# Turning a block's rows on the vector engine instead of TensorE, with the rows fetched in four partition groups and the later w1 loads issued by ScalarE

## The chip, the cores and the metric

The kernel runs on one core of a Trainium2 chip. The metric is the device time of one execution in microseconds; smaller is better. The core has five engines that run side by side: TensorE (PE in the profile; PEld is its weight load), VectorE (DVE), ScalarE (ACT), GpSimd (POOL) and SyncE (SP). SP computes nothing: it reads table entries into registers and issues DMA transfers. ScalarE and GpSimd can issue transfers too. Each engine works through its own instructions strictly in the order in which the program lists them, and waits on semaphores for the others.

## The reference

Two stages follow each other. The first is an attention without softmax: `q` and `k` are sketched into 64 features each, and the output is a ratio. The second is a mixture of experts: a noisy router picks two of eight experts for each of 4,352 rows, and each expert is a two-layer perceptron.

```python
def phi(x):
    a = np.einsum('rd,bhsd->bhsr', S1, x)
    b = np.einsum('rd,bhsd->bhsr', S2, x)
    return np.einsum('bhsi,bhsj->bhsij', a, b).reshape(*x.shape[:-1], r * r)
q_p, k_p = (phi(q), phi(k))
kv = np.einsum('bhsf,bhsd->bhfd', k_p, v)
z = np.sum(k_p, axis=2)
num = np.einsum('bhsf,bhfd->bhsd', q_p, kv)
den = np.einsum('bhsf,bhf->bhs', q_p, z)[..., None] + 1e-06
attn = num / den                     # 4 batches, 4 heads, 1088 rows, 32 wide
x = attn.transpose(0, 2, 1, 3).reshape(4352, 128)
...
noisy_logits = x @ w_gate + np.log1p(np.exp(x @ w_noise)) * noise
top2 = the two largest of the 8, top2_w = their softmax
for e in range(8):                   # w1[e] is 128 x 1024, w2[e] is 1024 x 128
    h = np.maximum(x[mask] @ w1[e], 0.0)
    out[mask] += top2_w[mask, k, None] * (h @ w2[e])
```

All of it is in float32.

## The kernel before

**Attention and router.** The four batches are worked through in turn. For each, TensorE turns and sketches k and q, VectorE multiplies the features, and a router step (`router`) finds the two experts of each row. The weight of the pick and the attention's denominator are multiplied into the row at once, so what a block later works on is already weighted. GpSimd scatters the rows, 128 at a time (L638), into a DRAM table `xs` that is sorted by expert. A row there is 129 words: 128 values and, as the last word, the id of the pair of row and expert.

**Blocks.** A block is 128 neighbouring rows of `xs` that belong to one expert. There are 72 in this part of the program, in six waves; a wave can begin as soon as enough rows have been routed. VectorE writes for each wave a small table `tab`, from which the expert and the first row of each block are read into a register (`value`, L762). With the order of blocks in the trace counted from 0, the waves begin at blocks 0, 5, 9, 17, 27 and 43.

For block b, `work_off` lists:
- `fetch_rows(b + 2)`: a load of 128 x 129 words from `xs` into a tile `xb`, issued by SP (L804). There are 11 such tiles; one is free again when GpSimd has scattered the block's result by the ids in the last column.
- `fetch_weights(b + 3)`: a load of the expert's w1, 128 x 1024 words, issued by SP (L796). There are four tiles; one is free again when TensorE has done its block.
- eight matmuls in two groups of four, w1 by the turned rows `bT`, into the PSUM tile `hp` (L981). In float32 each takes two slots of TensorE, so a group has 8. `hp` has two buffers. Each group is evicted through a ReLU into `h`: by ScalarE (L778), or, from block 27 on, the second group by VectorE (L776).
- `turn_input(b + 1)`, listed after the first of the two groups: TensorE transposes the 128 x 128 values of the next block's `xb` into PSUM (L885), and ScalarE copies them to the SBUF tile `bT` (L778).
- `second()`, two groups behind: the matmuls of `h` by w2, which stays in SBUF, into `acc` (L896). After a block's second one, `acc` is copied to `y` and GpSimd scatters it into the DRAM table `parts` (L929).

**Order.** The order on TensorE, ScalarE, VectorE and SP is the one in which the program lists the instructions (`manual_schedule`). Until block 27 or so the blocks are interleaved with attention and routing of later batches, step by step. While the last wave of rows is made ready, SP also writes eight pads of 128 x 129 words into `xs` (L767), one per block. In the last dozen blocks SP loads finished pairs from `parts` (`two`, L1036), VectorE adds the two halves of each row, and ScalarE and SP store them to `out` (L1042).

**Semaphores of transfers.** Transfers issued by SP and ScalarE share eight semaphores, which are given out in turn; a transfer waits for the earlier one that used the same semaphore.

Of the kernel before, what the change touches and what calls it, by code (L numbers as in the profile page):

```python
# [21 lines left out]
def kernel(  # L22
# [14 lines left out]
    nc = tc.nc  # L37
    V = nc.vector
    P = nc.NUM_PARTITIONS
    B, H, S, DH = q.shape  # L40
    R = S1.shape[0]
    D = H * DH
    E = moe_w_gate.shape[1]
# [23 lines left out]
    XW = D + 1  # L67
# [61 lines left out]
    ident = const.tile([P, P], F32, name="ident")  # L129
# [131 lines left out]
    xs = dram.tile([E * CAP + P, XW], F32, name="xs", tag="xs")  # L261
# [71 lines left out]
    def behind(name, i, step):  # L333

        for s_, writers in steps[name].items():
            if s_ > step:
                tc.declare_no_dep(i.ins, group=f"{name}{s_}", reason="rows of later steps")
            else:
                for w in writers:
                    tc.add_manual_dep(i.ins, w.name, SYNC, reason="reads what they write")  # L340
        tc.add_to_no_dep_group(name, i.ins)
# [303 lines left out]
    def send_all(step):  # L645
        send(sum(w[0] <= step for w in waiting))
# [111 lines left out]
    SP, PE, DVE, ACT, POOL = (getattr(mybir.EngineType, x) for x in ("SP", "PE", "DVE", "Activation", "Pool"))  # L758
    SPARE = 3

    def value(tab, w, at, most, engine=SP):
        return nc.values_load(tab[0:1, w, at:at + 1], engines=[engine], min_val=0, max_val=most,  # L762
                              skip_runtime_bounds_check_because="counts of pairs, clamped in the table")
# [6 lines left out]

    combining = {}
    W_AHEAD, X_AHEAD, LAG = 3, 2, 2

    def evict(o, i, vector, relu=False):
        if vector:
            V.tensor_scalar_max(o, i, 0.0) if relu else V.tensor_copy(o, i)  # L776
        else:
            nc.scalar.activation(out=o, in_=i, func=AF.Relu) if relu else nc.scalar.copy(o, i)  # L778

    def work_off(*waves, skip=0, most=None, at=None):  # L780
# [8 lines left out]
        weights, rows, ready, later = {}, {}, {}, []  # L789

        def fetch_weights(i):
            if i < n:
                tab, k = tabs[blocks[i][0]], blocks[i][1]
                w1 = weights[i] = wpool.tile([P, F], F32, name="w1", tag="w1")
                e = value(tab, 0, k, E - 1)
                nc.sync.dma_start(w1[:], moe_w1[bass.ds(e, 1), :, :].rearrange("o p f -> p (o f)"))  # L796

        def fetch_rows(i):
            if i < n:
                tab, (k, step) = tabs[blocks[i][0]], blocks[i][1:3]  # L800
                send_all(step)
                r = value(tab, 1, k, E * CAP)
                xb = rows[i] = xpool.tile([P, XW], F32, name="xb", tag="xb")
                behind("xs", nc.sync.dma_start(xb[:], xs[bass.ds(r, P), :]), step)  # L804

        def late(i):

# [74 lines left out]

        def turn_input(i, acc):

            nc.tensor.transpose(acc[:, P:2 * P], rows[i][:, 0:D], ident[:])  # L885
            xT = moe.tile([P, P], F32, name="bT", tag="bT")
            evict(xT[:], acc[:, P:2 * P], False)
            ready[i] = (xT, value(tabs[blocks[i][0]], 0, blocks[i][1], E - 1, PE))

        def accumulator():  # L890
            return ps_o.tile([P, 512], F32, name="acc", tag="acc")
# [49 lines left out]
        def combine_some(k):  # L941
# [15 lines left out]
            if k == LAST - SPARE - LATE - 1:  # L957
                combining["last"], = combine(last_parts[:, NT - FINAL:NT], last_out[:, NT - FINAL:NT], 2, FINAL, nc.sync, 1)
                next(combining["last"])

        fetch_weights(0)
        for i in range(X_AHEAD):
            fetch_rows(i)
        for i in range(1, W_AHEAD):
            fetch_weights(i)
        acc = accumulator()
        turn_input(0, acc)
        yield
        for b in range(n):

            for i in range(b + X_AHEAD, b + X_AHEAD + 1 + min(max(b - (n - 2 * LATE - 4), 0), LATE)):
                if i not in rows:
                    fetch_rows(i)
            fetch_weights(b + W_AHEAD)
            if b:
                acc = accumulator()
            w1, (xT, e), spread = weights.pop(b), ready.pop(b), blocks[b][3]
            for j0 in range(0, FJ, 4):
                hp = ps_h.tile([P, 512], F32, name="hp", tag="hp")
                for j in range(4):  # L980
                    nc.tensor.matmul(hp[:, P * j:P * (j + 1)], lhsT=w1[:, P * (j0 + j):P * (j0 + j + 1)],  # L981
                                     rhs=xT[:], start=True, stop=True)
                h = hpool.tile([P, 512], F32, name="h", tag="h")
                evict(h[:], hp[:], spread and j0 > 0, relu=True)
                later.append((acc, h, e, j0, b))
                if len(later) > LAG:
                    second()
                if j0 == 0 and b + 1 < n:
                    turn_input(b + 1, acc)
                at[0] = blocks[min(n - 1, b + 1 + W_AHEAD)][0] if j0 else 0  # L990
                yield
# [361 lines left out]
```

## Time and profile before

| | |
|---|---|
| time, median of 3 runs | 388.0 us (384.33 to 388.43) |
| the profiled run | 369.02 us, span on the core 367.1 us |
| TensorE busy | 349.4 us, 95% |
| VectorE, ScalarE, GpSimd busy | 155.6, 127.1 and 155.6 us (42%, 35%, 42%) |
| granted TensorE clock | 0.99 |
| turns of blocks on TensorE (L885) | 72, listed with 275 ns each |
| copies of the turned rows by ScalarE | 72, 265 ns each |
| loads of rows issued by SP | 72, 64.5 KB each |
| loads of w1 issued by SP | 72, 512 KB each |

The profile is a recording of one execution. Its page has the busy time of each engine, the span in 40 slices with the busy share in tenths, the DMA queues, and the costliest groups of instructions (line, engine, operation, tiles, how many; then busy time and mean ns of one; then the idle time of the engine just before them and who ended it). Matmuls overlap, so the listed time of one is longer than the distance to the next. Further views of the same recording give the instructions of one tile, all instructions in order of time (start, duration, engine, line, with the idle time before them in brackets), and the busy time of each engine in chosen stretches.

### The profile page before, as it was taken

Reading aid. Unit: us, or ns where it says so; the run is one execution under the profiler, and the core shown is the slowest. Engines: PE = TensorE matmul, PEld = TensorE weight load, DVE = VectorE, ACT = ScalarE, POOL = GpSimd, SP = SyncE. Lnnn points to the kernel's source line nnn. Section 1 sums busy time; section 2 is a strip of 40 time slices with the busy share of each in tenths; the row PEclk is TensorE's granted clock in tenths of the full one; section 3 lists DMA queues with packets and bytes.
Section 4 is the critical chain, followed back from the end, with each engine's and each line's share of the span. In section 5 each row is a group of like instructions: output and inputs, shape, how many; then the busy total and the mean of one; then the engine's idle time right before and its main releaser. Section 6 shows DMA issues by size and latency. Waiting matters only on the chain. (4 is left out here: it accounts for less than half of the span.)

```text
span 367.1 us, 9385 instructions
## 1 busy us (share of the span) xinstructions
PE 349.4 (95%) x3064; PEld 343.5 (94%) x3064; DVE 155.6 (42%) x557; ACT 127.1 (35%) x314; POOL 155.6 (42%) x216
## 2 busy tenths in 40 slices
PE   7998879999999999999999999999999999999990
PEld 7887779999999999999999999999999999999990
DVE  4759979335355160086602323232222222334650
ACT  3353342545544445554442121212222222222220
POOL 7002740367454577463756654323232323232352
PEclk9999998999999999999999999999999999999997
DMA  6799737657274465556588775656565657979651
GB/s 188 196 273 294 209 99 249 203 156 236 55 213 138 131 171 175 155 178 170 165 242 246 219 212 181 194 166 199 157 196 166 192 168 209 321 220 342 230 179 48
DMA packets 47231, 71.04 MB, mean 194 GB/s; under 512 B 10143, under 2 KB 32290, under 8 KB 47184
## 3 DMA queue, kind: packets, MB, share of 16 engines
q1 hardware_dynamic: 39216, 59.71, 55.3%
q0 software_dynamic: 4608, 9.07, 7.2%
q10 hardware_dynamic: 3360, 1.64, 1.5%
q8 instruction: 28, 0.46, 0.5%
q14 instruction: 19, 0.16, 0.1%
HBM read 58.25 MB, written 12.56 MB: 193 GB/s over the span
## 5 line engine op out<-in xcount | busy, mean ns | idle before, releaser
L981 PE MATMUL hp<-bT,w 128*128 128x128 f32 x1152 | 154.1, 277 | 0.0
L896 PE MATMUL acc<-w,h 128*128 x1152 | 152.0, 275 | 0.0
L981 PEld LDWEIGHTS hp<-bT,w 128*128 128x128 f32 x1152 | 140.9, 193 | 0.5
L896 PEld LDWEIGHTS acc<-w,h 128*128 128x128 f32 x1152 | 140.1, 192 | 0.0
L929 POOL DMA_INDIRECT parts<-y,xb x68 | 69.8, 1026 | 147.3 <-DVE y L776 79.0
L778 ACT ACTIVATE h<-hp 128x512 f32<-128x512 f32 x99 | 59.1, 597 | 143.3 <-PE hp L981 133.8
L638 POOL DMA_INDIRECT xs<-xg,to x68 | 70.1, 1030 | 46.1 <-DVE co L562 25.6
L776 DVE TENSOR_SCALAR h<-hp 128x512 f32<-128x512 f32 x45 | 31.1, 692 | 109.0 <-PE hp L981 109.0
L778 ACT COPY bT<-acc 128x128 f32<-128x128 f32 x72 | 19.1, 265 | 25.5 <-PE acc L885 25.1
L382 DVE TENSOR_TENSOR phi<-ab 128x1024 f32<-128x1024 f32 (+1 forms) x18 | 20.5, 1137 | 0.6
L885 PE MATMUL acc<-ident,xb 128*128 128x128 f32 x72 | 19.8, 275 | 0.9 <-DMA xb<-xs 0.9
L776 DVE COPY y<-acc 128x128 f32<-128x128 f32 x41 | 12.0, 292 | 10.4 <-PE acc L896 9.9
L418 PE MATMUL bank<-vld,phi 128*128 128x96 f32 x128 | 15.7, 280 | 0.5 <-DVE phi L382 0.5
L418 PEld LDWEIGHTS bank<-vld,phi 128*128 128x128 f32 x128 | 15.4, 198 | 0.6 <-DVE phi L382 0.6
L362 PE MATMUL bank<-sk,xT 128*128 128x128 f32 x102 | 13.6, 281 | 1.2 <-ACT xT L357 0.8
L362 PEld LDWEIGHTS bank<-sk,xT 128*128 128x128 f32 x102 | 12.3, 194 | 1.8 <-ACT xT L357 1.3
L778 ACT COPY y<-acc 128x128 f32<-128x128 f32 x30 | 8.0, 265 | 13.0 <-PE acc L896 13.0
L377 DVE TENSOR_TENSOR ab<-bank,ab 128x256 f32<-128x256 f32 (+1 forms) x15 | 5.6, 374 | 15.4 <-ACT ab L369 15.4
L504 DVE TENSOR_SCALAR den<-nd 128x16 f32<-128x16 f32 (+2 forms) x5 | 0.9, 179 | 25.1 <-ACT nd L478 25.1
L576 DVE TENSOR_TENSOR xg<-nd,co 128x256 f32<-128x256 f32 (+2 forms) x20 | 11.3, 605 | 0.5 <-issue 0.2
L885 PEld LDWEIGHTS acc<-ident,xb 128*128 128x128 f32 x72 | 10.4, 145 | 1.1 <-DMA xb<-xs 1.1
L357 ACT COPY xT<-bank 128x512 f32<-128x512 f32 (+1 forms) x15 | 7.5, 526 | 7.4 <-PE bank L355 7.4
(204 smaller groups left out, 262.1 us busy)
## 6 DMA issues: line engine op xcount, KB each, us to landing
w<-in_moe_w_dram SPq DMA_DIRECT2D x72, 512.0 KB
xb<-xs SPq DMA_DIRECT2D x72, 64.5 KB
two<-parts SPq DMA_DIRECT2D x8, 384.0 KB
kld<-in_k_dram SPq DMA_DIRECT2D x4, 512.0 KB
qld<-in_q_dram SPq DMA_DIRECT2D x4, 512.0 KB
vld<-in_v_dram SPq DMA_DIRECT2D x8, 256.0 KB
out_dram<-two ACTq DMA_DIRECT2D x8, 192.0 KB
xs<-xg,to POOLq DMA_INDIRECT x68
```

The lines of the kernel that those rows point to most:

```text
L357: nc.scalar.copy(self.xT[:, 0:P * self.n], ps[:, 0:P * self.n])
L362: nc.tensor.matmul(ps[:, P * i:P * (i + 1)], lhsT=self.xT[:, P * i:P * (i + 1)], rhs=sk[:].rearrange("p i h y -> p (i h y)"), start=True, ...
L382: yield V.tensor_tensor(out=self.phi[:, 0:n].rearrange("p t h (i j) -> p (t h) i j", i=R), in0=th[:, :, 0, :].unsqueeze(3).to_broadcast([P ...
L418: nc.tensor.matmul(ps[:, W * hp:W * (hp + 1)], lhsT=lhsT, rhs=rhs, start=(t == 0 and hp == 0), stop=(t == NT), skip_group_check=True)
L576: return V.tensor_tensor(out=xg[:, i, 0:n, 2 * DH * hp:2 * DH * (hp + 1)].rearrange("p t (h d) -> p t h d", h=2), in0=x[:, :, hp, 0:2 * (D ...
L638: x = nc.gpsimd.indirect_dma_start(out=xs[:], out_offset=bass.IndirectOffsetOnAxis(ap=to[:, i, t:t + 1], axis=0), in_=xg[:, i, t, :], in_o ...
L776: V.tensor_scalar_max(o, i, 0.0) if relu else V.tensor_copy(o, i)
L778: nc.scalar.activation(out=o, in_=i, func=AF.Relu) if relu else nc.scalar.copy(o, i)
L885: nc.tensor.transpose(acc[:, P:2 * P], rows[i][:, 0:D], ident[:])
L896: nc.tensor.matmul(acc[:, 0:D], lhsT=h[:, P * j:P * (j + 1)], rhs=w2[:, bass.ds(FJ * e + (j0 + j), 1), :], start=(j0 + j == 0), stop=(j0 + ...
L929: sent = nc.gpsimd.indirect_dma_start(out=parts[:], out_offset=bass.IndirectOffsetOnAxis(ap=rows.pop(i)[:, D:XW].bitcast(U32), axis=0), in ...
L981: nc.tensor.matmul(hp[:, P * j:P * (j + 1)], lhsT=w1[:, P * (j0 + j):P * (j0 + j + 1)], rhs=xT[:], start=True, stop=True)
```

## The change

The turn of a block's rows leaves TensorE. VectorE can turn squares of 32 x 32 values inside a tile, in place of the whole 128 x 128. So that this gives the full turn, the rows are fetched in another order: the load of one 128 x 129 piece becomes four, each of which fills 32 partitions. Partition 32i + b of `xb` then holds, for j = 0 to 3, columns 32i to 32i + 31 of row 32j + b. Each run of 32 values is 128 bytes. When VectorE turns each of the sixteen squares in place, the tile is the transpose of the rows. A fifth load fetches the ids into the last column as before. TensorE has 72 transposes less, and ScalarE 72 copies from PSUM to SBUF less.

As SP now issues five transfers for a block's rows, the loads of w1 are issued by ScalarE, except for those of the first three blocks of each wave, whose table may not be ready yet.

```diff
+    TURN = 32
...
                 w1 = weights[i] = wpool.tile([P, F], F32, name="w1", tag="w1")
-                e = value(tab, 0, k, E - 1)
-                nc.sync.dma_start(w1[:], moe_w1[bass.ds(e, 1), :, :].rearrange("o p f -> p (o f)"))
+                engine, queue = (ACT, nc.scalar) if k >= W_AHEAD else (SP, nc.sync)
+                e = value(tab, 0, k, E - 1, engine)
+                queue.dma_start(w1[:], moe_w1[bass.ds(e, 1), :, :].rearrange("o p f -> p (o f)"))
...
                 xb = rows[i] = xpool.tile([P, XW], F32, name="xb", tag="xb")
-                behind("xs", nc.sync.dma_start(xb[:], xs[bass.ds(r, P), :]), step)
+                x = xs[bass.ds(r, P), :]
+                for i_ in range(P // TURN):
+                    c = slice(TURN * i_, TURN * (i_ + 1))
+                    behind("xs", nc.sync.dma_start(xb[c, 0:D].rearrange("b (j a) -> b j a", a=TURN),
+                                                   x[:, c].rearrange("(j b) a -> b j a", b=TURN)), step)
+                behind("xs", nc.sync.dma_start(xb[:, D:XW], x[:, D:XW]), step)
...
         def turn_input(i, acc):
-            nc.tensor.transpose(acc[:, P:2 * P], rows[i][:, 0:D], ident[:])
             xT = moe.tile([P, P], F32, name="bT", tag="bT")
-            evict(xT[:], acc[:, P:2 * P], False)
+            V.transpose(xT[:], rows[i][:, 0:D])
             ready[i] = (xT, value(tabs[blocks[i][0]], 0, blocks[i][1], E - 1, PE))
```

In the program that results, each turn on VectorE waits for the landings of its four pieces. It stands where the copy stood in the order: after the eviction of the first group of the block before.

## The prediction

> **What bounds the kernel now.** I read the page's busy times and slices first, then the windows, then the timeline of one block in the middle of the longest wave.
>
> ```profile
> PE 349.4 (95%) x3064; PEld 343.5 (94%) x3064; DVE 155.6 (42%) x557; ACT 127.1 (35%) x314; POOL 155.6 (42%) x216
> PE   7998879999999999999999999999999999999990
> L885 PE MATMUL acc<-ident,xb 128*128 128x128 f32 x72 | 19.8, 275 | 0.9 <-DMA xb<-xs 0.9
> ```
> ```profile
> 188.00:340.00 152.00, 152.00 (x1364) 152.00 (x1363) 43.07 (x93) 36.32 (x85) 53.59 (x54) 1.00 0.71 214
> ```
> ```profile
> 234.44 0.27 PE L885 MATMUL acc<-ident,xb 128*128 128x128 f32 x1
> 234.44 0.97 PEld L981 LDWEIGHTS hp<-bT,w 128*128 128x128 f32 x8
> 234.55 1.06 PE L981 MATMUL hp<-bT,w 128*128 128x128 f32 x8
> 234.75 0.27 ACT L778 COPY bT<-acc 128x128 f32<-128x128 f32 x1 [0.34 <-PE acc L885]
> ...
> 235.63 0.33 SPq L796 DMA_DIRECT2D w<-in_moe_w_dram  x1
> ...
> 236.71 0.33 SPq L804 DMA_DIRECT2D xb<-xs  x1
> ...
> 238.12 0.27 PE L885 MATMUL acc<-ident,xb 128*128 128x128 f32 x1
> ```
>
> TensorE has no gap from 55 us, where the first block starts, to 351 us, where the last one does: it is the bound, and all else lies beside it. The timeline gives its true price. The turn (L885) is listed with 0.27 us, but the next matmul starts 0.11 us after it, and a block repeats every 3.68 us (234.44 to 238.12) with 33 slots (16 L981, 16 L896, one turn): 3.68/33 = 0.1115 us a slot. So the 19.8 us of the group are not 19.8 us of time.
>
> **What the Trainium skill says.** "Trainium Kernel Development and Optimization", Performance Expectations, calls matmul busy time a bad metric because matmuls are pipelined; the trace agrees (275 ns listed, 111 ns apart). "VectorE: DVE Perf Modes", The three transpose paths: the vector engine turns 32x32 squares only, 311 ns for 128x128 in bf16; no row of this trace shows the instruction. "DMA: Bandwidth & Descriptors", Issuing engines are not separate DMA queues: a second issuing engine saves only the issuing sequencer's time; here an issue takes 0.33 us. The same page, Specifications, wants 512 B or more a piece for line rate. The trace's packet records agree in direction: 28 ns for a 516 B packet, 13 ns for 128 B, 9 ns for 4 B.
>
> **The change part by part.**
>
> Removed from TensorE: 72 turns of 0.1115 us = 8.0 us, all on the path. A block becomes 3.57 us.
>
> Removed from ScalarE: 72 copies of 0.265 us = 19.1 us. It was 24% busy from 188 us on: no time. Added to it: 54 w1 loads (the first three of each of six waves stay on SP), each a table read (0.27 us on SP), register work and an issue (0.38 us for its out_dram stores), about 0.9 us. Behind such a load on ScalarE stands the eviction of h (0.60 us), and hp has two buffers, so TensorE waits for it only 2.65 us after hp is done (three groups of 8 slots). 0.9 + 0.6 fits; the load's buffer is freed by a group of matmuls that ends 1.8 us before this hp. In the last dozen blocks the load also waits for landings of SP's transfers; this I price with the end phase below.
>
> Added to VectorE: 72 turns. Nearest rows: 0.29 us for a 128x128 copy; the skill's 0.31; at half rate for four-byte elements 0.6. I take 0.3: 21.6 us on an engine that is 42% busy, 28% in the long wave (43.07 of 152): hidden. Each waits for four landings, and behind it stand router steps and, from block 27 on, the eviction of h's second half. TensorE needs the result three groups (2.65 us) later. VectorE's bursts between two turns stay under that except in the last table (five steps of 0.94 us): 0.3 us.
>
> Transfers: a block's rows were 128 packets of 516 B, 128 x 28/16 = 0.22 us on each of 16 engines; they become 512 of 128 B and 128 of 4 B, (512 x 13 + 128 x 9)/16 = 0.49 us. 0.27 us more of 3.57 us on a DMA share of 0.71 gives 0.79: hidden. If each 128 B packet took as long as a 516 B one, +0.75 us, 0.92: still hidden.
>
> Added to SP, where the cost is: five issues a block in place of one.
>
> ```profile
> L804 SPq DMA_DIRECT2D xb<-xs x72: 332/333/564, 53.0 to 330.9; - x72
> ```
> ```profile
> L187 SPq DMA_DIRECT2D v_rest<-in_v_dram x8: 595/611/617, 4.2 to 42.7; - x8
> ```
> ```profile
> L200 SPq DMA_DIRECT2D wgn<-in_moe_w_noise_dram x2: 425/426/426, 9.9 to 10.4; - x2
> ```
> ```profile
> 182.47 0.52 SPq L804 DMA_DIRECT2D xb<-xs  x1
> 183.56 0.33 SPq L796 DMA_DIRECT2D w<-in_moe_w_dram  x1
> 184.39 0.36 SPq L767 DMA_DIRECT2D xs<-pad  x1
> 185.31 0.34 SPq L804 DMA_DIRECT2D xb<-xs  x1
> ```
>
> The first three lines give minimum, median and maximum of the issue in ns. A 128-row load costs 0.333; v_rest has the new pieces' 128 packets of 128 B but 64 rows, 0.611; wgn has their 32 rows, 0.35 to 0.43. The fourth is SP's own order in a wave start: each transfer with its table read costs about 0.88 us. **The unknown is the issue of one piece, p, between 0.333 and 0.611 us.** 32 rows are the nearer likeness, and other loads of wgn's time also took 0.42 to 0.51 where later ones of their shape took 0.33, so I take p = 0.38. A piece without a table read adds about 0.16 us of register and semaphore work (37 + 29 + 17 ns and gaps). A block's rows then cost SP (0.86 - 0.333 + p) + 3 (p + 0.16) + 0.49 = 3.0 us. That is under 3.57 only because w1 left SP; with w1 it would be 3.9. SP no longer stands behind w1's wait for TensorE, so it can run ahead: in the middle of a wave nothing is lost. What is lost is at the places where SP starts without a lead:
> - Block 0: TensorE already waits for xb (0.9 us). Three more pieces, 1.6 us, less what TensorE can do meanwhile: 1.0.
> - Blocks 5 and 6: rows first at 78.1 us, TensorE at 83.0; the four pieces are usable at 81.9; block 6 just in time: 0.
> - Blocks 27 to 34: eight pads stand between, and w1 of the first three stays on SP. Rows of 27 issued from 182.5 to 185.0, then twice 0.88 + 0.88 + 3.0 and five times 3.9: 214.0. A load is usable some 1.5 us after its issue (block 0: 53.0 to 54.8), the turn takes 0.3, and the id is not waited for: 215.3. TensorE would be there at 188.5 + 7 x 3.57 = 213.5: 1.8.
> - The end phase, 12 loads of two among the last rows (18 us of lead before): 0.5.
>
> Sum: -8.0 + 0.3 + 1.0 + 1.8 + 0.5 = -4.4 us. The timed runs are 1.05 times the profiled one (388.0 against 369.0 us); scaled, -4.6 us: **383.4 us.**
>
> **The rivals.**
> - *All is hidden:* p is 0.333 to 0.35, or SP's lead suffices. For it: 32-row loads down to 0.35. -8.0 x 1.05: 379.6 us.
> - *The gain is given back in waits for rows:* p = 0.43, as wgn's median. Rows 3.2 us a block; blocks 27 to 34 lose 3.4, block 0 1.2, the end 2.5, VectorE's order 1: 8.1 against 8.0, so 388 us.
> - *SP becomes the bound, slower:* p = 0.54, as 64-row loads of two (0.51 to 0.58). Rows cost 3.66 us, over TensorE's 3.57, and SP never regains a lead. Rows of 27 end at 185.5, two blocks of 5.42, five of 4.54, 37 of 3.66, 8 us for two: 362.4, usable 363.7, where TensorE starts its last block at 351.4 now: +12.3, scaled 401 us. At 0.611 the same sum gives +25, 414 us. For it: every 64-row load is slow, so issue time isn't packets alone. Against: wgn.
>
> **How the numbers follow.** Forecast 0.40, all hidden 0.13, given back 0.21, SP the bound 0.26. Of the forecast's spread a fifth lies within 1%. Faster by over 1% (under 384.1): 0.48. Within 1%: 0.23. Slower: 0.29, SP's case and a tail of given back. The range runs from 378.5, just under all hidden, to 401, SP's middle case; its upper half up to 414 is left out, with some 0.05 below.
>
> **What would show it.** Right: a repeat of 3.57 us a block, no L885, a turn on VectorE near 0.3 us, xb issues of 0.33 to 0.43 us, and TensorE's idle gaps, waiting for VectorE's turn and behind it for xb, near blocks 0 and 27 to 34 only, 3 to 4 us in all. Wrong: xb pieces of 0.5 us or more with SP issuing without pause and a block at SP's pace; or ScalarE's h held up by its w1 loads and TensorE waiting for hp; or a turn of over 0.6 us.

## The result, and the profile after

The changed kernel takes 416.4 us (median of four runs, 413.3 to 422.0), the kernel before beside it 386.2 us. The ratio is 1.075, with a 95% interval of 1.063 to 1.087: slower by 30 us, where 4.6 us less were forecast. Ratios leave out runs that took over 1.5% longer than the fastest of the same kernel, here the one of 422.0.

The page of the kernel after, its busy times, its slices, and the groups that answer to those of before (the first line is the first-layer matmuls of the kernel before):

```profile
L981 PE MATMUL hp<-bT,w 128*128 128x128 f32 x1152 | 154.1, 277 | 0.0
```
```profile
PE 363.6 (87%) x2992; PEld 352.6 (85%) x2992; DVE 173.2 (42%) x629; ACT 106.0 (25%) x242; POOL 153.3 (37%) x216
...
PE   8998679978999996999996889999989799885792
...
PEclk9997769998999996999998999999999999999698
...
L989 PE MATMUL hp<-bT,w 128*128 128x128 f32 x1152 | 159.9, 283 | 28.2 <-issue 16.3
...
L779 ACT ACTIVATE h<-hp 128x512 f32<-128x512 f32 x99 | 58.9, 598 | 208.1 <-PE hp L989 89.4
...
L895 DVE STREAM_TRANSPOSE bT<-xb 128x128 f32<-128x128 f32 x72 | 22.0, 306 | 80.7 <-DMA xb<-xs 66.1
```

TensorE no longer runs in one piece: the row of nines of before now has sixes, sevens and eights among the blocks, and the first-layer matmuls (L989) stand 28.2 us idle where they stood 0.0. The last group tells who is late: the turn itself is short (306 ns), but VectorE idles 66.1 us ahead of it for rows. Next the issues of the rows (minimum, median and maximum in ns; L811 are the four pieces, L813 the ids), and the windows of the stretch that was shown of before (columns: sum, PE, PEld, DVE, ACT and POOL busy, clock, DMA share, GB/s):

```profile
L811 SPq DMA_DIRECT2D xb<-xs x288: 3/317/1567, 52.5 to 383.5; - x144
...
L813 SPq DMA_DIRECT2D xb<-xs x72: 11/352/1235, 55.0 to 384.1; - x72
```
```profile
188.00:340.00 152.00, 138.19 (x1187) 135.02 (x1187) 49.41 (x139) 27.28 (x51) 55.75 (x56) 0.99 0.67 176
```

A piece costs SP 0.317 us, less than forecast, and the DMA share is 0.67 against 0.71: no single issue is dear, and the DMA engines are not full. In the timeline a block in an undisturbed place repeats after 3.57 us, as worked out:

```profile
262.69 1.06 PE L989 MATMUL hp<-bT,w 128*128 128x128 f32 x8
...
266.26 0.94 PE L989 MATMUL hp<-bT,w 128*128 128x128 f32 x7
```

The waits (engine, tile and line, what ended them; us in total, how often, longest) show two chains, the first of transfers into the turn, the second of transfers into ScalarE's evictions. In the kernel before ScalarE's evictions had only these of any length behind transfers:

```profile
ACT h L778 <- DMA out_dram<-two: 5.6, 2, 3.1
...
ACT h L778 <- DMA w<-in_moe_w_dram: 2.5, 1, 2.5
```

In the kernel after:

```profile
DVE bT L895 <- DMA xb<-xs: 66.1, 27, 6.2
...
ACT h L779 <- DMA xb<-xs: 34.4, 9, 5.4
...
ACT h L779 <- DMA w<-in_moe_w_dram: 22.3, 7, 4.1
...
PE hp L989 <- ACT h L779: 8.4, 8, 2.2
```

An eviction needs neither rows nor weights. It waits because a w1 load stands ahead of it on ScalarE, and that load waits for an earlier transfer on its semaphore. The timeline shows one such case:

```profile
301.27 0.35 ACTq L799 DMA_DIRECT2D w<-in_moe_w_dram  x1
...
301.73 0.60 ACT L779 ACTIVATE h<-hp 128x512 f32<-128x512 f32 x1 [4.94 <-DMA xb<-xs]
...
302.37 1.16 PE L989 MATMUL hp<-bT,w 128*128 128x128 f32 x8 [1.56 <-ACT h L779]
```

The w1 load has the semaphore of a piece that SP issued at 298.16 us and that landed at 301.14. Only then is it issued. The eviction follows 3.6 us after the last matmul of its `hp` ended (298.13 in the same timeline), and TensorE has lost 1.56 us.

**The account.** The changed kernel is compared with another profile of the kernel before from a chip of like speed (a_before below). From the first block to the last group of first-layer matmuls it takes 337.9 us against 304.5, 33.4 more. Gaps of TensorE are 36.6 us against 6.3: +30.3. (A gap is here the distance from the start of one matmul to the start of the next, less one slot of 0.1115 us, so it is a little longer than the idle time that a view lists.) By the work that ended last before each gap, some 18 us of them are behind the turn and some 13 behind ScalarE's h. The clock is at half for 20.5 us of the stretch (windows at 94.7, 159.6 to 166.4, 224.4 and 384.9 to 391.7) against none. TensorE stands still in 2.7 us of that, and half of the rest is lost: about +9. The turns removed: 72 x 0.1115 = -8.0. The sum is about +31; the other 2 us stay unaccounted for. By place, the larger gaps of the kernel after are 4.8 us at 85 to 110, 4.0 at 155 to 160 (2.2 of such gaps were there before), 9.1 at 180 to 250, 7.0 at 280 to 335 and 10.5 at 360 to 390.

Some chips ran the kernel before in 386 to 388 us and others in 367; each ratio is to the kernel before on the same chip, and times of different chips are not set against each other.

### The profile page after: what moved, and what is told of

It is laid out like the page before. It is cut to its first block, busy times and chain, and to the rows that moved or that the text cites. A ratio compares the mean times of both kernels' runs of the same rounds, so it can differ in the third digit from the quotient of the medians.

```text
span 416.0 us, 10178 instructions
## 1 busy us (share of the span) xinstructions
PE 363.6 (87%) x2992; PEld 352.6 (85%) x2992; DVE 173.2 (42%) x629; ACT 106.0 (25%) x242; POOL 153.3 (37%) x216
## 4 chain that ended last, share of the span: by engine, by line
PE 62%; DMA 10%; issue 9%; DVE 7%; SPq 6%; ACT 2%; another core or an unknown queue 1%; POOL 1%; ACTq 0%; DVEq 0%; POOLq 0%
PE hp L989 24%; PE acc L904 21%; PE bank L418 5%; SPq L811 4%; DMA xb<-xs 4%; DMA w<-in_moe_w_dram 3%; PE bank L475 2%; PE bank L362 2%; PE acc L475 2%; DMA late<-parts,mates 1%; PE acc L458 1%; DMA two<-parts 1%; PE bank L458 1%; ACT h L779 1%
## 5 line engine op out<-in xcount | busy, mean ns | idle before, releaser
L989 PE MATMUL hp<-bT,w 128*128 128x128 f32 x1152 | 159.9, 283 | 28.2 <-issue 16.3
L989 PEld LDWEIGHTS hp<-bT,w 128*128 128x128 f32 x1152 | 144.0, 196 | 33.2 <-issue 22.0
L904 PE MATMUL acc<-w,h 128*128 x1152 | 155.5, 279 | 0.0
L904 PEld LDWEIGHTS acc<-w,h 128*128 128x128 f32 x1152 | 143.5, 196 | 0.2 <-issue 0.2
L895 DVE STREAM_TRANSPOSE bT<-xb 128x128 f32<-128x128 f32 x72 | 22.0, 306 | 80.7 <-DMA xb<-xs 66.1
L382 DVE TENSOR_TENSOR phi<-ab 128x1024 f32<-128x1024 f32 (+1 forms) x18 | 20.5, 1137 | 0.6
L418 PE MATMUL bank<-vld,phi 128*128 128x96 f32 x128 | 18.5, 311 | 0.5 <-DVE phi L382 0.5
L475 PE MATMUL bank<-kv,phT 128*128 128x98 f32 (+1 forms) x72 | 10.1, 303 | 3.7 <-issue 3.7
L475 PEld LDWEIGHTS bank<-kv,phT 128*128 128x128 f32 (+1 forms) x72 | 9.3, 213 | 4.2 <-issue 4.0
L475 PE MATMUL acc<-kv,phT 128*128 128x98 f32 (+1 forms) x72 | 9.5, 299 | 0.8 <-ACT kv L442 0.5
L475 PEld LDWEIGHTS acc<-kv,phT 128*128 128x128 f32 (+1 forms) x72 | 9.2, 212 | 1.1 <-ACT kv L442 0.6
```

The costliest lines, as they stand in the source:

```text
L382: yield V.tensor_tensor(out=self.phi[:, 0:n].rearrange("p t h (i j) -> p (t h) i j", i=R), in0=th[:, :, 0, :].unsqueeze(3).to_broadcast([P ...
L418: nc.tensor.matmul(ps[:, W * hp:W * (hp + 1)], lhsT=lhsT, rhs=rhs, start=(t == 0 and hp == 0), stop=(t == NT), skip_group_check=True)
L475: nc.tensor.matmul(ps[rows, c0:c0 + YC], lhsT=self.phT[hp][:, P * i + rows.start:P * i + rows.stop], rhs=kv[:, hp, :], start=True, stop=True)
L895: V.transpose(xT[:], rows[i][:, 0:D])
L904: nc.tensor.matmul(acc[:, 0:D], lhsT=h[:, P * j:P * (j + 1)], rhs=w2[:, bass.ds(FJ * e + (j0 + j), 1), :], start=(j0 + j == 0), stop=(j0 + ...
```

## The experiments

In the table are all kernels, in order of the transfers that a block needs (rows and ids, and w1), as SP and ScalarE issue them from a wave's fourth block on.

| kernel | SP + ScalarE | what | ratio (95%) |
|---|---|---|---|
| before | 2 + 0 | | 1 |
| b_one_load_w_sp | 2 + 0 | turn on VectorE, one load of rows | 0.988 (0.982 to 0.992) |
| c_one_load_w_act | 1 + 1 | the same, w1 by ScalarE | 0.988 (0.984 to 0.992) |
| f_sixteen | 2 + 0 | one load, sixteen single squares | 1.210 (1.199 to 1.221) |
| i_two_w_act | 2 + 1 | two loads of 64 rows | 0.996 (0.993 to 0.999) |
| r_every_second | 2 or 6, + 0 | the change in 19 of 72 blocks | 0.997 (0.994 to 0.999) |
| j_four_w_act | 4 + 1 | four loads of 32 rows with ids | 1.039 (1.032 to 1.046) |
| d_four_plain_w_act | 5 + 1 | the change, whole rows | 1.081 (1.076 to 1.086) |
| g_first_whole | 5 + 1 | one load of rows, four small ones after it | 1.073 (1.065 to 1.080) |
| after; m_after_again | 5 + 1 | the change | 1.075; 1.075 (1.071 to 1.078) |
| h_w_after_h; n_h_again | 5 + 1 | w1 listed behind h | 1.080; 1.085 (1.079 to 1.090) |
| q_x_ahead | 5 + 1 | rows four blocks ahead | 1.071 (1.062 to 1.079) |
| t_ids_pool | 5 + 1 | copies of ids off VectorE | 1.095 (1.092 to 1.099) |
| o_split_w_act | 3 + 3 | two pieces by ScalarE | 1.079 (1.072 to 1.086) |
| p_split_w_sp | 4 + 2 | the same, w1 by SP | 1.043 (1.035 to 1.051) |
| s_split_ahead | 4 + 2 | p with rows four blocks ahead | 1.043 (1.036 to 1.050) |
| e_four_w_sp | 6 + 0 | all by SP | 1.128 (1.120 to 1.136) |

**The parts alone.** First the kernel before again, for a second profile; then the turn on VectorE with one load of whole rows, w1 by SP (b) or by ScalarE (c). Both leave out the exchange of squares, so `bT` holds each square turned but in the wrong place. Against the changed kernel:

```diff
-                for i_ in range(P // TURN):
...
-                behind("xs", nc.sync.dma_start(xb[:, D:XW], x[:, D:XW]), step)
+                behind("xs", nc.sync.dma_start(xb[:], xs[bass.ds(r, P), :]), step)
```

> The kernel before, once more, for its profile. The two profiles at hand differ by 10 us before the first block starts (first L981 or L989 matmul at 56.0 and 66.2 us), in a part of the program that the change doesn't touch, with half the TensorE clock granted for 17 us of the changed kernel's first 61 us and for 3.4 us of the other's. If that is chance, this profile shows windows of half clock too, at other places than the first one, and a span between 367 and 387 us. If it belongs to the change, the first block starts at 56 us again with a clock of 0.99.

> The turn on VectorE alone: rows in one load as before, w1 issued by SP as before. Left out: the exchange of the squares outside the diagonal, so the rows that the matmuls see are permuted. What every theory expects: TensorE loses 72 slots of 0.1115 us and nothing is added to SP, so 8 us less than before, ratio 0.98, block repeat 3.57 us. If a turn on VectorE or its place in the order costs by itself, the ratio is 1.0 or more.

> As b_one_load_w_sp, with the later w1 loads issued by ScalarE; the same part is left out. Theory A (w1's issue on ScalarE, standing before the eviction of h, is what costs): 10 to 20 us over b_one_load_w_sp, with TensorE waiting for ScalarE's h. Theory B (it costs only because five small transfers a block use up the eight semaphores, so that w1's issue waits for recent landings): with two transfers a block the wait is for a landing four blocks back, so within 2 us of b_one_load_w_sp. Theory C (late landings of rows alone): the same as b_one_load_w_sp.

Measured: 383.3 us for the kernel before (one run), 381.1 for b and 381.1 for c beside 385.7. The turn's move is worth 1.2%, 4.6 us, and ScalarE's issuing of w1 costs no time as long as there are two transfers a block. All of the loss comes with the four pieces and the load of ids. ScalarE's evictions are held in c too, for 13.8 us behind transfers of rows, but too briefly to stop TensorE for long; the changed kernel has 34.4 and 22.3 (w1). The turn waits for rows for 9.9 us, where the changed kernel has 66.1:

```profile
ACT h L779 <- DMA xb<-xs: 13.8, 4, 3.7
...
DVE bT L890 <- DMA xb<-xs: 9.9, 3, 5.7
```

**Packets or the number of transfers.** d takes the four loads and the id load, but each loads 32 whole rows; j drops the id load from that, i has two loads of 64 rows with their ids. All three leave out the exchange.

```diff
-                    behind("xs", nc.sync.dma_start(xb[c, 0:D].rearrange("b (j a) -> b j a", a=TURN),
-                                                   x[:, c].rearrange("(j b) a -> b j a", b=TURN)), step)
+                    behind("xs", nc.sync.dma_start(xb[c, 0:D], x[c, 0:D]), step)
```

> As the changed kernel, but each of the four loads takes 32 whole rows (32 packets of 512 B in place of 128 of 128 B); the exchange of squares is left out as in b_one_load_w_sp. If the number of transfers is what costs (theories A, B and C): within 8 us of the changed kernel, ratio 1.05 to 1.08 to before. If the size of the packets costs (theory D): most of the loss goes, ratio under 1.02.

> As d_four_plain_w_act, with two loads of 64 whole rows, ids included, so three transfers a block with w1's in place of six; the exchange of squares is left out. Eight semaphores then reach back over 2.7 blocks and SP's cost is about 1.7 us a block. Theories B and C alike: as c_one_load_w_act, ratio 0.985 to 0.995. If each further transfer costs its landing on the path: about 8 us over c_one_load_w_act, a quarter of the way to d_four_plain_w_act.

> Four loads of 32 whole rows, the ids in them: five transfers a block in place of d's six. The exchange of squares is left out. If every further transfer costs alike, and two loads (three transfers) were 0.996 and d (six) 1.081, five transfers give 1.05 on a straight line from three. If there is a knee where the rows' issues pass what a wave start or the semaphores leave, it is under 1.03. If the id load alone is dear (128 packets of 4 B), also under 1.03.

d is as slow as the changed kernel, with packets of 512 bytes in place of 128: packets are not the cause. Three transfers a block give 0.996, five 1.039, six 1.07 to 1.08. j lies a little under the straight line from three to d (1.053), so the last transfer seems to cost more than the ones before it; i, j and d ran on three different chips, and the intervals of j and of the line nearly touch. "DMA: Bandwidth & Descriptors", Rules for kernel authors, of the Trainium skill, says to join many small transfers, since under 64 KB one pays mostly overhead. The runs agree: by the packet records a 16 KB piece is 128 x 13 ns / 16 = 0.1 us of data, and lands 2.8 us after its issue (median; nine in ten within 4.1).

**Late pieces or SP's pace.** In g the block's own rows come in one load, first; four loads of 32 x 32 follow into a tile that nothing reads. The exchange is left out.

```diff
+                behind("xs", nc.sync.dma_start(xb[:], x[:]), step)
+                spare = spool.tile([P, TURN], F32, name="spare", tag="spare")
...
+                    behind("xs", nc.sync.dma_start(spare[c, :], x[c, 0:TURN]), step)
-                behind("xs", nc.sync.dma_start(xb[:, D:XW], x[:, D:XW]), step)
```

> A block's rows come in one load of 128 whole rows with their ids, the first of the block; four small loads of 32 x 32 into a buffer that nothing reads follow it, so a block has six transfers again (five by SyncE, w1 by ScalarE), but the block's own rows no longer land last. The exchange of squares is left out. If SyncE's pace and the shared completion semaphores cost the time (a transfer has to wait for the landing of an earlier one): about as d, ratio 1.06 to 1.09, with VectorE's turns waiting some 20 us for rows. If it is the late landing of a block's last piece: near c, 0.99 to 1.01. If it is the small packets or the bytes: near c as well, since the small loads carry little.

1.073: transfers that nobody waits for, with hardly any bytes, cost as much as the pieces. What costs is that they are issued at all.

**All issues on SP, and w1 behind the eviction.** e is the changed kernel with every w1 on SP. h and n list the w1 load behind the first eviction of h, and m repeats the changed kernel beside n.

```diff
-            fetch_weights(b + W_AHEAD)
...
                 evict(h[:], hp[:], spread and j0 > 0, relu=True)
+                if j0 == 0:
+                    fetch_weights(b + W_AHEAD)
```

> The changed kernel with all w1 loads issued by SP, as before. A block then costs SP 3.0 + 0.9 = 3.9 us, over TensorE's 3.57. Theory C (SP's pace and landings): slower than the changed kernel by 0.3 to 0.5 us for each of 45 blocks, 10 to 25 us, ratio 1.10 to 1.14, with all gaps ending at the turn. Theory B (ScalarE's wait is the greater part): 5 to 12 us faster than the changed kernel.

> The changed kernel with the w1 load listed behind the eviction of h's first group instead of ahead of it. In the changed kernel's blocks TensorE's gaps sum to 36.6 us: 18.1 end with VectorE's turn, 12.8 with ScalarE's eviction of h. Theory B (the w1 load, waiting for a landing on a shared semaphore, holds up the eviction behind it): the 12.8 us go and most of them come back as time, 8 to 13 us less than the changed kernel, ratio about 1.05. Theory C (SP's pace and the rows' landings set the blocks' pace and the held eviction only hides it): within 4 us of the changed kernel.

> The changed kernel again, for the same chip as the next one and for a profile of another execution: ratio 1.075 to 1.10. TensorE's gaps among the blocks: some 37 us, half of them behind VectorE's turns and a third behind ScalarE's h.

> The changed kernel with a w1 load listed behind the first eviction of h, beside the changed kernel on one chip. If ScalarE's held evictions are a part of the loss of their own: 0.02 to 0.03 under the changed kernel's ratio (12.8 us of TensorE's gaps are theirs). If they only stand in for the late rows: within 0.01 of it.

e is slowest but one, 1.128: with six issues SP is behind almost everywhere, and the turn waits 139.6 us for rows. Another 12.6 us of TensorE's gaps, after 354 us, wait for w1 itself, which SP now issues there among the combine's loads.

```profile
DVE bT L895 <- DMA xb<-xs: 139.6, 51, 5.7
```

The changed kernel repeats (1.075). n is not faster than m but slower, 1.085 against 1.075. In the two profiles TensorE's gaps behind ScalarE fall from 13.0 to 9.6 us, and those behind the turn rise from 21.3 to 25.7. But the edit didn't free the evictions: they stand behind rows and w1 for 37.0 + 7.7 us in m and for 42.0 + 29.4 in n. So this pair doesn't tell whether held evictions are a part of the loss of their own.

**SP or the shared semaphores.** o and p keep the six transfers and their semaphores, but ScalarE issues two of the four pieces (o), and SP gets all w1 back (p). q changes only how far ahead rows are listed; s does this to p.

```diff
+                x2 = xs[bass.ds(value(tab, 1, k, E * CAP, ACT), P), :]
...
-                    behind("xs", nc.sync.dma_start(
+                    queue, x = (nc.sync, x) if i_ < 2 else (nc.scalar, x2)
+                    behind("xs", queue.dma_start(
...
```
```diff
-    W_AHEAD, X_AHEAD, LAG = 3, 2, 2
+    W_AHEAD, X_AHEAD, LAG = 3, 4, 2
```

> The changed kernel with two of a block's four pieces issued by ScalarE: as many transfers over the same completion semaphores, but SyncE issues three a block and ScalarE three (its w1 load among them). If SyncE's own pace is what costs the time: ratio 0.98 to 1.02, SyncE idle again for a third of the long wave. If the semaphores and landings shared by six transfers a block cost it: 1.06 to 1.09, as the changed kernel. If ScalarE's issues now hold up h: 1.03 to 1.06, with TensorE's gaps behind ScalarE's h.

> The same split, with every w1 load on SyncE: four transfers a block there, two on ScalarE. If SyncE's pace decides: between o and the five-transfer kernel (1.039), 1.00 to 1.04. If the semaphores decide: 1.06 to 1.09 again.

> The changed kernel with rows listed four blocks ahead in place of two. If the loss is SyncE's order, rows standing behind its waits for w1 and for the combine's loads near the end (some 13 us there): 1.04 to 1.05. If it is SyncE's pace, which an order cannot change: 1.07 to 1.08.

> The split of p_split_w_sp (two pieces by ScalarE, every w1 by SyncE) with rows listed four blocks ahead. If the late rows and ScalarE's held evictions are two parts that add: p without the turns' 9 us, 1.01 to 1.03. If they stand for one another, as with q_x_ahead: 1.04 to 1.06, with the gaps behind ScalarE's h.

Only s does what one of its expectations said (1.04 to 1.06, gaps behind ScalarE's h); o has the ratio of one and the gaps of another, p lies just above its range, and q hits a range for another reason. In o the gaps behind the turn fall to 3.3 us at most, as SP's pace would have it, but those behind ScalarE's h rise to 28.7: the ratio stays. The waits of o, then of p, then of q:

```profile
ACT h L779 <- DMA xb<-xs: 118.0, 34, 7.3
...
DVE bT L897 <- DMA xb<-xs: 39.3, 17, 5.9
```
```profile
ACT h L779 <- DMA xb<-xs: 69.5, 21, 6.9
...
DVE bT L897 <- DMA xb<-xs: 65.6, 33, 5.8
```
```profile
ACT h L779 <- DMA xb<-xs: 58.7, 18, 6.5
...
ACT h L779 <- DMA w<-in_moe_w_dram: 24.6, 8, 4.4
...
DVE bT L895 <- DMA xb<-xs: 6.3, 5, 2.7
```

In q the turn hardly waits (6.3 us, 66.1 in the changed kernel), ScalarE waits more, and the ratio is the same, 1.071. That equality is in part chance. At the second block TensorE stands 6.1 us for a w1 load that SP now issues behind the rows of two more blocks, and 10.2 us at half clock begin there:

```profile
PE hp L989 <- DMA w<-in_moe_w_dram: 6.1, 1, 6.1
```

The first three blocks take 26.1 us in q and 18.7 in t (below), on the same chip. Part of what earlier rows gained is given back there, so the equal ratio doesn't show that the loss only changed its place.

In s as in p the ratio is 1.043, with the gaps behind the turn down from 6 us to 2 and those behind ScalarE's h up from 10 to 12. So there are two costs, and moving issues trades one for the other. On SP, in the long wave, it is the issuing itself: in the 129 us from 205 to 334 SP waits for only 5.8 us in the changed kernel, 0.9 in m and 6.5 in e, and rows come late because five or six issues a block take its time. On ScalarE it is the wait for landings: an issue stands still until the earlier transfer on its semaphore has landed, and evictions stand still behind it. The division has a better and a worse point: 4 + 2 is better than 5 + 1, 3 + 3 and 6 + 0. No run changed the number of semaphores, so what more of them would give is not shown.

**Single squares.** f keeps one load, all w1 on SP, and turns sixteen squares one by one straight to their places.

```diff
-            V.transpose(xT[:], rows[i][:, 0:D])
+            for r in range(0, P, TURN):
+                for c in range(0, D, TURN):
+                    V.transpose(xT[c:c + TURN, r:r + TURN], rows[i][r:r + TURN, c:c + TURN])
```

> Rows in one load, w1 by SP, and VectorE turns the sixteen squares one by one, each to its own place, so the whole reference is computed. If a square takes about 0.1 us beside its neighbours, VectorE has 1.6 us more a block, 2.6 of 3.57 us in the long waves, and the kernel is as b_one_load_w_sp or up to 8 us over it: ratio 0.99 to 1.01. If it takes 0.19 us, as the smallest dependent steps of the router, VectorE needs 4 us a block and becomes the bound: ratio 1.06 or more.

```profile
L892 DVE STREAM_TRANSPOSE bT<-xb 32x32 f32<-32x32 f32 x1152 | 233.2, 202 | 16.0
```

One square takes 202 ns, all sixteen of a tile in one instruction 306. In this profile (of a run of 452.8 us; the three others took 443.0 to 449.6) VectorE is busy 141.1 of the 152 us from 188 to 340, with a block every 4.4 us in the long wave: it has become the bound.

**The end phase.** The largest gap of the changed kernel, 4.9 us before block 68, has VectorE standing at copies of the ids of the last four blocks, which wait for landings and stand ahead of that block's turn. t gives these copies to GpSimd.

```diff
-                    V.tensor_copy(one(ids, late(i)), rows[i][:, D:XW].bitcast(U32))
+                    nc.gpsimd.tensor_copy(one(ids, late(i)), rows[i][:, D:XW].bitcast(U32))
```

> The changed kernel with the copies of the last four blocks' ids (one column each) made by GpSimd in place of VectorE. In the changed kernel they stand ahead of the turn of block 68 on VectorE, wait for the ids of blocks 68 to 71 until 386 us, and TensorE has a gap of 4.9 us there. If the turn's place behind VectorE's own waits costs that: the gap goes and the half clock behind it, 5 to 8 us less, ratio 1.054 to 1.062. If the rows would be late anyway: 1.07 to 1.08, with the gap behind block 68's rows.

A miss: 1.095. The single gap is gone, but the last blocks have five gaps of 0.6 to 2.0 us behind the turn in its place, 6.5 us in all. They stand behind VectorE's additions for the combine, which wait for their own loads from SP (6.6 and 4.9 us in two cases). Why the ratio is above the 1.071 that q had on this chip stays open; the changed kernel itself was not run on it.

**A part of the change.** r turns on VectorE only every second block from a wave's fifth on, not among the last 14 of all, and leaves w1 to SP. This came to 19 blocks.

```diff
+        def squares(i):
+            step, k = blocks[i][0:2]
+            return k >= 4 and k % 2 == 0 and not (step == STEPS - 1 and k >= LAST - 14)
...
```

> Only every second block, from the fifth of a wave on and not among the last 14 of all, is turned by VectorE from four pieces; the others keep the one load and TensorE's turn, and SyncE issues every w1. If only the number of issues on SyncE and on the shared semaphores costs the time: SyncE's mean is (0.86 + 3.0)/2 + 0.88 = 2.8 us a block against 3.6, so nothing is lost and some 25 turns of 0.11 us are saved: 0.99 to 1.00. If any block of four pieces loses by itself: 1.02 to 1.04.

0.997 (0.994 to 0.999), by 0.3% faster than the kernel before, the interval just clear of no change. 19 x 0.1115 = 2.1 us or 0.6% were to be had. Its page has TensorE's row of nines again, and its turn hardly waits:

```profile
PE   8998889999999999999999999999999999999980
...
L903 DVE STREAM_TRANSPOSE bT<-xb 128x128 f32<-128x128 f32 x19 | 5.7, 301 | 0.3 <-DMA xb<-xs 0.3
```

A block of four pieces is thus not slow by itself. Which of r's restraints keeps it so is not told apart: every second block, no block at the start of a wave or among the last 14, and w1 on SP.

## Why the prediction was wrong

**Right in its sizes.** The slot of 0.1115 us (3.57 us a block where nothing waits); the turn, taken as 0.3 us, measured 0.306; the piece, taken as 0.38, measured 0.317; the DMA engines as no bound; ScalarE's issue of w1 as such, free in c. The gain of 8.0 us was there too: c takes 3.6 us less than a_before from the first block to the last (300.9 against 304.5), which is -8.0, +2.4 of gaps and +1.7 of one window at half clock.

**Not shown: block 0, 1.0 us.** It starts at 66.2 us against 65.1 in a_before, but b and c, which fetch the rows in one load, start it at 66.0 and 65.9.

**Wrong: "A load is usable some 1.5 us after its issue".** This was read from block 0, where nothing else was under way. Among the blocks a load of whole rows took a median of 3.2 us from issue to landing even in the kernel before (nine in ten within 4.7), and w1 3.8; I had the trace and took one unloaded case. The pieces of the changed kernel land after 2.8.

**Wrong: "0.9 + 0.6 fits".** The term priced ScalarE's w1 load by its instructions and put its wait for landings into the last dozen blocks only. With six transfers a block, eight semaphores reach back 1.3 blocks, less than 5 us; with two they reach back four. So a w1 load meets transfers that SP has just issued anywhere; in the case shown ScalarE stood idle for 4.94 us. The 3.6 us that `hp` waited and 0.6 for the eviction make 4.2, over TensorE's tolerance of 2.65 by the 1.56 that it lost. Cost: some 13 us of gaps behind ScalarE's h, 6.7 of them in the middle of the long wave (300 to 335 us), where "nothing is lost" was forecast. Of the others, 3.7 lie in the end phase and count there again below.

**Mis-sized: blocks 5 and 6, 0.** Their ids, the last of a block's five transfers, were issued 2.1 and 0.7 us before TensorE started the block; in the kernel before, the rows were issued 4.9 and 6.9 ahead. The turn of block 5 waits 4.4 us for its pieces. Cost: 3.9 us of gaps and a window at half clock.

**Mis-sized: blocks 27 to 34, 1.8 us.** From the rows of block 27 to those of block 34 SP was forecast at 29.0 us (twice 4.76, five times 3.9) and took 34.0 (4.9, 7.5, then 3.9 to 4.9), waits included, one of them 2.2 us:

```profile
SPq L813 <- DMA w<-in_moe_w_dram: 2.2, 1, 2.2
SPq L811 <- DMA w<-in_moe_w_dram: 1.0, 1, 1.0
SPq L811 <- DVE bT L895: 0.7, 3, 0.3
SPq L799 <- PE hp L989: 0.7, 1, 0.7
```

These are the longest waits of SP between 205 and 334 us: all eight that are listed add to 5.8 us of 129. SP issues without pause, which is the mechanism of the rival "SP becomes the bound", at a piece of 0.317 us where that rival wanted 0.54. The ids are issued 2.6 to 5.9 us before TensorE starts the block from 27 to 45; in the kernel before the rows were issued 6.0 to 10.9 ahead. A lead of about one landing is no lead. Cost: of the 9.1 us of gaps from 180 to 250, 7.8 are behind the turn, at blocks 28 to 34.

**Mis-sized: the end phase, 0.5 us.** 10.5 us of gaps. SP stands 18.2 us at the combine's loads, 8.7 in one piece, with rows queued behind (8.7 us in all before, at most 3.7 in one piece); and the turn is now on VectorE, which also adds the combine's pairs. I asked what is queued behind the turn, and not what the turn is queued behind.

```profile
SPq L1044 <- DMA parts<-y,xb: 18.2, 3, 8.7
```

**Not in the sum at all: the clock.** Gaps of over 2 us are often followed by windows at half clock, some 9 us lost here (below). Nor was the factor 1.05 from profiled to timed runs a scale. The profiled run of 369.0 us lies with the chips of 367, the timed ones with those of 386 to 388. In the profile from such a chip (a_before) TensorE stands 8.7 us behind ScalarE ahead of 52.7 us, the clock is at half for 13.7 us, and the first block starts at 65.1 us, against 56.0. The change touches none of this.

Of what the prediction named as signs against itself, one came, h "held up by its w1 loads and TensorE waiting for hp", and half of another: "SP issuing without pause", but with pieces of 0.317 us and not of 0.5.

## What to carry to other kernels

Count transfers, not bytes: add up the time that the issuing engine needs for all of a block's issues, and for every transfer added, ask who waits for its semaphore next, how many transfers ago that was first used, and what stands behind the waiting issue on its engine; take landing times from the loaded part of the trace. Moving issues to another engine helps only if nothing urgent is queued behind them there. Before work moves to another engine, read that engine's order for what the work will stand behind, and where a stretch of the program can bear the cost, make the change there alone.

## What the runs showed of the hardware

Between the first and the last, the stretches of TensorE's clock in these profiles are multiples of 3.4 us (3.413 or 6.827 at half clock in the changed kernel), and a gap often costs more than its length. In the 20 profiles, after 80 us and up to the last block, with gaps taken from the start of one matmul to the start of the next, 3 of 169 gaps of 0.8 to 2 us were followed by half clock, 24 of 53 gaps of 2 to 3 us, and 23 of 28 longer ones; 47 of the 48 stretches at half clock, of one or more windows, followed a gap of over 2 us. "TensorE: Matmul & The Clock Gate", Part 1, of the Trainium skill, gives the same window (3413 ns) and half clock after an idle one; here gaps well under a window often were enough. A busy window at half clock loses half of 3.4 us, 1.7, so by this estimate a gap of 2.5 us can cost 4.2.

A single 32 x 32 turn on VectorE takes 202 ns, two thirds of the 306 ns that sixteen of them take in one instruction.
